# First maxima of an attention block: their keys and queries loaded ahead of block 3's stores, and their visits spread over all remaining projections

## The chip, the cores and the metric

The kernel runs on one core of a Trainium2 chip. The metric is device time in microseconds (us), the median of several runs. Five engines matter: TensorE (PE in the profile, with its weight loads as PEld), VectorE (DVE), ScalarE (ACT), GpSimd (POOL) and SyncE (SP), which here only issues DMAs. Each engine works through its own instructions in order.

## The reference

One transformer block with adaptive layer norm, for 2048 tokens of width 512, 32 heads of width 16:

```
mod = (silu(c) @ w_mod) -> sa, ca, ga, sb, cb, gb
h = layernorm(x) * (1 + ca) + sa
q, k, v = split(h @ wqkv);  p = softmax(q @ k.T / 4) per head
x = x + ga * ((p @ v) @ wo)
h = layernorm(x) * (1 + cb) + sb
x = x + gb * (gelu(h @ w1 + b1) @ w2 + b2)
```

All in float32. A softmax needs for each query the maximum of its scores, and the kernel works these maxima out by matmuls of their own.

## The kernel before, in words

**Parts.** Tokens come in four blocks of 512 (`b`), heads in eight groups of four (`g`); a *unit* `u` is one group with one block of queries, `u = 4 * g + block`. There are three parts. The first (lines 615 to 672) normalises and transposes the blocks and makes the projections of keys and queries of the first 128 channels (`k = 0`: `w = 1` keys, `w = 0` queries) and seven of the sixteen token tiles of values. The second (lines 681 to 755) makes the 33 remaining projections, called *items*: nine value tiles, then `k` = 1 to 3 for each block, keys and queries. In between the matmuls of the items it makes the maxima of the first nine units, in the order of `FRONT` (0, 1, 2, 3, 4, 5, 8, 6, 7). The third part is the attention with the remaining maxima, and after it the feed-forward network. Only the first two parts are edited.

**Projections.** An item is twelve matmuls of line 304 (four chunks, each with high and low parts in three products). `proj_qk` and `proj_v` take a list `fill` of functions that are spread evenly between these twelve. Both return a closure `rest`, which stores the result; it is called later, as the first element of the next item's `fill`. Results go to DRAM (`qk_d`, `v_d`) as high and low parts, and are loaded back in the shape that the scores need.

**Maxima of the front.** For the first nine units keys are not used one by one. For pairs of blocks the kernel stores the sum and the difference of their keys (`kpm_d`, from tiles `pm` and `pmh`, made in `proj_qk` when `pair and b % 2`). The larger of two scores is then |difference| + sum: kind "V" is a matmul with one of the two and an absolute value on ScalarE (line 573), kind "U" a matmul with the other and a combined add and minimum on VectorE (line 576). Both matmuls are line 567, with 48 rows; two row groups (`a` = 0, 1) lie beside each other. Of each unit there are 16 V and 16 U for each row group. `slots` lists them so that a U follows its V, and a *visit* takes three slots, six matmuls. There are 97 visits. The first two units alternate, and their first 16 pairs use only the first half of the keys (blocks 0 and 1).

**Where visits lie.** `FILL0 = 3`: the first three items have none, and the 97 are spread over the other 30, three or four to an item:

```
m, nm = n - FILL0, len(items) - FILL0
fill = [lambda rest=rest: (rest(), visit())] + [visit] * (visits * (m + 1) // nm - visits * m // nm - 1)
```

**Loads.** Keys of the front lie in two tiles `kts[0]` and `kts[1]` (`kt` in the profile), queries in `qmx` (two buffers). Groups 0 and 2 use `kts[0]`, group 1 `kts[1]`: group 2's are loaded at item 19, once group 0 is done. All are loaded by six small DMAs each (`build_k`, line 498; `build_q`, line 509) from SP's queue; in block 3 and the second part the stores go there too (`st[0] = sy`), before that mostly to ScalarE's. The queue is worked in program order, and a DMA that must wait holds up all behind it. The memory of `kts` and `qmx` is that of the input tiles of the first part (`lcm` is closed at block 3), so their loads wait for the last transposes (line 261). `load_qm` of the next unit is issued when the current one is two pairs old, and waits until TensorE has finished with the unit before.

In block 3 the order on SP's queue is: queries of unit 0; block 3's keys; its sum and difference; the first half of the group's keys; queries of unit 1. The second half of the keys follows in items 2 to 4, two DMAs each.

Of the kernel before, what the change touches and what calls it, by code (L numbers as in the profile page):

```python
# [7 lines left out]
F32 = mybir.dt.float32  # L8
# [3 lines left out]
ALU = mybir.AluOpType  # L12
# [5 lines left out]
S = 2048  # L18
# [7 lines left out]
TB = S // NB  # L26
# [9 lines left out]

FRONT = (0, 1, 2, 3, 4, 5, 8, 6, 7, 9)
NU1 = len(FRONT) - 1
FILL0 = 3
VISIT = 3  # L40
OP0 = 1
OPN = 4
# [11 lines left out]
def block_kernel(ctx: ExitStack, tc: tile.TileContext, x, wqkv, wo, w1, b1, w2, b2, c, w_mod, out):  # L54
    nc = tc.nc
    te, ve, ac, gp, sy = nc.tensor, nc.vector, nc.scalar, nc.gpsimd, nc.sync
# [368 lines left out]
    def proj_qk(b, k, w, fill=(), ps=None):  # L425
        hi, lo = hT[b]
        if ps is None:
            ps = bank()
            mm3(ps, [w_hi[k][:, w, i] for i in range(KC)], [w_lo[k][:, w, i] for i in range(KC)],
                [hi[:, i] for i in range(KC)], [lo[:, i] for i in range(KC)], fill)  # L430
        parts = tpool.tile([P, 2, TB], FR, tag="parts", name="parts", bufs=5)
        pair = w and k < 2
        if k or b == 0 or pair and b % 2 == 0:
            raw = tpool.tile([P, TB], F32, tag="raw", name="raw", bufs=3)
            ac.activation(raw, ps, AF.Copy)  # L435
            if pair:
                k2[b % 2] = raw
        if k or b == 0:
            gp.tensor_copy(parts[:, 0], raw)
            gp.tensor_tensor(parts[:, 1], raw, parts[:, 0].bitcast(F32), op=ALU.subtract)  # L440
        else:
            ac.activation(parts[:, 0], ps, AF.Copy)
            ve.tensor_tensor(parts[:, 1], ps, parts[:, 0].bitcast(F32), op=ALU.subtract)
        if pair and b % 2:
            pm = [tpool.tile([P, TB], F32, tag="pm", name="pm", bufs=1), k2[0]]
            pmh = [tpool.tile([P, 2, TB], FR, tag="parts", name="pmh", bufs=5) for _ in range(2)]
            if not k:
                for i, op in enumerate((ALU.add, ALU.subtract)):
                    ve.tensor_tensor(pm[i], ps, k2[0], op=op)
                    ac.activation(pmh[i][:, 0], pm[i], AF.Copy)  # L450

        def pair_store():
            for i in range(2):
                t0 = (b - 1 + i) * TB
                st[0].dma_start(kpm_d[k][:, :, t0 : t0 + TB].rearrange("a p t -> p a t"), pmh[i].bitcast(F32))

        def rest():
            st[0].dma_start(qk_d[w][k][:, :, b * TB : (b + 1) * TB].rearrange("a p t -> p a t"), parts.bitcast(F32))
            if pair and b % 2:
                for i, op in enumerate((ALU.add, ALU.subtract)):  # L460
                    if k:
                        gp.tensor_tensor(pm[i], k2[1], k2[0], op=op)
                        gp.tensor_copy(pmh[i][:, 0], pm[i])
                    eng = gp if k else ve
                    eng.tensor_tensor(pmh[i][:, 1], pm[i], pmh[i][:, 0].bitcast(F32), op=ALU.subtract)
                if k:
                    new.extend([lambda: None, pair_store])
                else:
                    pair_store()

        return rest
# [39 lines left out]
    def load_qm(u):  # L511

        qmx[u] = qmpool.tile([P, 2, TB], FR, tag="qmx", name="qmx", bufs=2)
        build_q(u, qmx[u])
# [105 lines left out]
    rest = lambda: None  # L620
# [8 lines left out]
    for b in range(NB):  # L629
        if b == NB - 1:  # L630
            close(lcm)
            kcm, kpool = pool("kpool")
            kts = [kpool.tile([P, 2, S], FR, name=f"kt{i}") for i in range(2)]
            qmcm, qmpool = pool("qmpool")
            kpm[0], kpm[1] = kts
            load_qm(0)
        if b:
            if b + 1 < NB:
                xn = ln1(b + 1)()
            if b + 2 < NB:  # L640
                load_x(b + 2)
        proj(proj_qk, b, 0, 1, (), None if b else first[1])
        if b == 1:
            load_w(1)
        if b == NB - 1:
            st[0] = sy
            rest()
            rest, st[0] = lambda: None, ac
            build_k(kts[0], kpm_d[0], 0, 0, 2 * TB)
            load_qm(1)  # L650
            split_w(1)
        elif b == 1:
            rest()
            rest = lambda: None
        proj(proj_qk, b, 0, 0, (), None if b else first[0])
        if b == 0:
            xn = ln1(1)()
        if b == NB - 1:
            mod_store(mrow)
            break  # L660
        if b == 1:
            mod_cols(1, mrow)
        for _ in range(V_A[b][0]):
            proj(proj_v, *vitems.pop(0), (), len(vitems) == 15)
        ev = ln1_t(b + 1, xn)
        ev()
        for _ in range(V_A[b][1]):
            proj(proj_v, *vitems.pop(0))
        if b < 2:
            mrow = mod_rows(wms)  # L670
        if b == 0:
            wms = [load_wm(2, 0), load_wm(5, 1)]
# [16 lines left out]
    visits = -(-len(slots) // VISIT)  # L689
# [11 lines left out]
    for n, (k, b, w) in enumerate(items):  # L701
        if n == 1:
            close(acm)
            st[0] = sy
        if 1 < n < 5:
            build_k(kts[0], kpm_d[0], 0, 2 * TB, S, (n - 2,))
        if n == 5:
            load_w(2)
        if n == 7:
            build_k(kts[1], kpm_d[0], 1)  # L710
            for t in kts:
                one_rows(t)
        if n == nv + 1:
            close(vwcm)
            kqcm, kqpool = pool("kqpool")
            kq = [kqpool.tile([P, 2, S], FR, name="kq0")]
            one_rows(kq[0])
            vgcm, vgpool = pool("vgpool", bufs=2)
            qcm, qpool = pool("qpool")
        if n == nv + 2:  # L720
            load_k(0, kq[0])
        if n == nv + 10:
            kpm[2] = kts[0]
            build_k(kts[0], kpm_d[1], 2)
        if n == nv + 15:
            load_v(0)
        if n == nv + 19:
            load_k(2, kts[0])
        if n == nv + 18:
            load_q(0)  # L730
        if n == nv + 20:
            load_q(1)
        if k and b == 1 and w and k < 3:
            split_w(k + 1)
            if k + 2 < 4:
                load_w(k + 2)
        new = []
        fill = [rest]
        if n >= FILL0:
            m, nm = n - FILL0, len(items) - FILL0  # L740
            fill = [lambda rest=rest: (rest(), visit())] + [visit] * (visits * (m + 1) // nm - visits * m // nm - 1)
        if n == len(items) - 1:
            fill += [lambda: None] * 2
        rest = proj_qk(b, k, w, fill) if k else proj_v(b, w, fill)
        for f in todo[:1]:
            f()
        todo = todo[1:] + new
# [386 lines left out]
```

## Time and profile before

| | |
|---|---|
| median of 3 runs | 1742.93 us (1739.42 to 1745.06) |
| the profiled execution | 1743.35 us, span 1741.6 us |
| granted TensorE clock, mean | 0.996 |
| busy | TensorE 99%, VectorE 80%, ScalarE 78%, GpSimd 18% |
| the second part | about 72 to 283 us of the span |

Times in the profile are from the span's start. A row of a timeline gives start, duration, engine, line, operation, what it writes and reads, and a count where several instructions are merged; in brackets how long its engine was idle before it, and what ended that. `SPq` is the queue of SP, and its rows are the issues of DMAs, not their landings. A busy TensorE is not TensorE at its peak: the ends of matmuls are modelled.

### The profile page before, as it was taken

Reading aid. Unit: us, or ns where it says so; the run is one execution under the profiler, and the core shown is the slowest. Engines: PE = TensorE matmul, PEld = TensorE weight load, DVE = VectorE, ACT = ScalarE, POOL = GpSimd, SP = SyncE. Lnnn points to the kernel's source line nnn. Section 1 sums busy time; section 2 is a strip of 40 time slices with the busy share of each in tenths; the row PEclk is TensorE's granted clock in tenths of the full one; section 3 lists DMA queues with packets and bytes.
Section 4 is the critical chain, followed back from the end, with each engine's and each line's share of the span. In section 5 each row is a group of like instructions: output and inputs, shape, how many; then the busy total and the mean of one; then the engine's idle time right before and its main releaser. Section 6 shows DMA issues by size and latency. Waiting matters only on the chain.

```text
span 1741.6 us, 28898 instructions
## 1 busy us (share of the span) xinstructions
PE 1729.5 (99%) x10560; PEld 900.4 (52%) x10560; DVE 1394.6 (80%) x2563; ACT 1351.9 (78%) x2582; POOL 317.4 (18%) x347
## 2 busy tenths in 40 slices
PE   9999999999999999999999999999999999999998
PEld 7655554343433433434343343433433488888887
DVE  6489999898888888888888888888886296746553
ACT  3478888999999999999999999999999732222222
POOL 3205531010000000000000000000013154645562
PEclk9999999999999999999999999999999999999999
DMA  8767657512300400500410111101023064423331
GB/s 305 236 136 166 165 131 149 106 38 43 65 22 19 84 23 23 88 23 24 78 32 24 39 33 26 39 23 36 23 64 102 22 199 125 140 78 116 97 121 49
DMA packets 125218, 144.15 MB, mean 83 GB/s; under 512 B 39026, under 2 KB 74866, under 8 KB 123124
## 3 DMA queue, kind: packets, MB, share of 16 engines
q1 hardware_dynamic: 121620, 135.21, 31.2%
q10 hardware_dynamic: 3456, 7.10, 1.1%
q8 instruction: 83, 1.36, 0.3%
q14 instruction: 59, 0.48, 0.1%
HBM read 106.37 MB, written 35.87 MB: 82 GB/s over the span
## 4 chain that ended last, share of the span: by engine, by line
PE 95%; DVE 2%; DMA 1%; ACT 0%; SPq 0%; POOL 0%; issue 0%; ACTq 0%
PE pv L802 29%; PE mx L548 20%; PE sc L304 15%; PE sc L969 14%; PE mx L1033 6%; PE mx L567 5%; PE pv L1033 2%; PE sc L909 2%; PE mx L909 1%; DMA qk<-parts 0%; PE sc L261 0%; DMA kt<-kpm 0%; PE sc L357 0%; DMA wmod<-in_w_mod_dram 0%; DVE mxs L550 0%; DMA v<-vst 0%
## 5 line engine op out<-in xcount | busy, mean ns | idle before, releaser
L970 ACT ACTIVATE p<-sc 128x512 f32<-128x512 f32 x2048 | 1054.8, 615 | 39.7 <-PE sc L969 13.6
L550 DVE TENSOR_REDUCE mxs<-mx 128x1 f32<-128x512 f32 x1472 | 927.6, 684 | 113.9 <-PE sc L969 79.3
L802 PE MATMUL pv<-p,vg 128*32 128x512 f32 x4096 | 546.0, 605 | 0.0
L969 PE MATMUL sc<-qst,kq 50*128 50x512 f32 x1024 | 284.0, 435 | 0.8 <-ACT raw L435 0.8
L969 PE MATMUL sc<-qst,kt 50*128 50x512 f32 x1024 | 282.4, 431 | 0.0
L548 PE MATMUL mx<-kq,qmx 48*128 48x512 f32 x768 | 262.1, 428 | 0.2
L548 PEld LDWEIGHTS mx<-kq,qmx 48*128 48x128 f32 x768 | 122.6, 184 | 228.6 <-DVE mxs L550 209.3
L548 PE MATMUL mx<-kt,qmx 48*128 48x512 f32 x704 | 239.7, 427 | 0.0
L548 PEld LDWEIGHTS mx<-kt,qmx 48*128 48x128 f32 x704 | 113.2, 184 | 208.3 <-DVE mxs L550 190.7
L1012 ACT ACTIVATE g<-sc,b_c 128x512 f32<-128x512 f32 x56 | 38.6, 690 | 222.7 <-PE sc L304 218.2
L576 DVE CUSTOM_DVE_ANT_0 cp<-mx,cp 128x512 f32<-128x512 f32 x288 | 182.8, 687 | 24.8 <-PE mx L567 21.0
L589 POOL CAST m<-mn 128x16 fp32r<-128x16 f32 x32 | 6.3, 197 | 1016.2 <-DVE mn L583 1016.2
L573 ACT ACTIVATE cp<-mx 128x512 f32<-128x512 f32 x288 | 151.7, 602 | 36.0 <-PE mx L567 35.6
L802 PEld LDWEIGHTS pv<-p,vg 128*32 128x32 f32 x4096 | 81.1, 108 | 180.7 <-issue 169.1
L969 PEld LDWEIGHTS sc<-qst,kq 50*128 50x128 f32 x1024 | 125.7, 185 | 32.9 <-ACT p L970 23.8
L1016 DVE TENSOR_TENSOR glo<-g,ghi 128x512 fp32r<-128x512 f32 x56 | 57.6, 1029 | 92.1 <-ACT ghi L1015 92.1
L969 PEld LDWEIGHTS sc<-qst,kt 50*128 50x128 f32 x1024 | 125.6, 185 | 10.0 <-ACT p L970 3.1
L567 PE MATMUL mx<-kt,qmx 48*128 48x512 f32 x576 | 102.4, 444 | 1.9 <-DMA qmx<-qk 1.7
L838 POOL TENSOR_TENSOR w1l<-w1r,w1h 128x512 fp32r<-128x512 f32 x56 | 76.5, 1366 | 146.7 <-DVE w1h L837 123.1
L840 POOL TENSOR_TENSOR w2l<-w2r,w2h 128x512 fp32r<-128x512 f32 x56 | 82.4, 1472 | 6.2 <-DVE w2h L839 5.8
L567 PEld LDWEIGHTS mx<-kt,qmx 48*128 48x128 f32 x576 | 55.3, 187 | 52.3 <-DVE mxf L576 25.6
L304 PE MATMUL sc<-kt,w1h 128*128 128x512 f32 x224 | 73.8, 391 | 0.0
(175 smaller groups left out, 1667.6 us busy)
## 6 DMA issues: line engine op xcount, KB each, us to landing
w1r<-in_B_w_dram SPq DMA_DIRECT2D x56, 256.0 KB
w2r<-in_B_w_dram SPq DMA_DIRECT2D x56, 256.0 KB
qk<-parts SPq DMA_DIRECT2D x25, 512.0 KB
qmx<-qk SPq DMA_DIRECT2D x192, 64.0 KB
qst<-qk SPq DMA_DIRECT2D x192, 64.0 KB
kq<-qk SPq DMA_DIRECT2D x24, 256.0 KB
kt<-qk SPq DMA_DIRECT2D x24, 256.0 KB
vg<-v SPq DMA_DIRECT2D x8, 664.0 KB
```

The source lines that it names most:

```text
L304: te.matmul(ps, p, q, start=i == 0, stop=i == len(terms) - 1)
L548: te.matmul(ps, qmx[u][rows, p, qc * P : (qc + 1) * P], kst[u // NB][rows, p, kr * TB : (kr + 1) * TB], start=True, stop=True)
L550: ve.tensor_reduce(mxs[u][:, p, a, qc, kr : kr + 1], ps, axis=AX.X, op=ALU.max, negate=True)
L567: te.matmul(ps, qmx[u][rows, p, qc * P : (qc + 1) * P], kpm[u // NB][rows, p, t0 : t0 + TB], start=True, stop=True)
L573: ac.activation(vabs[n, a], ps, AF.Abs)
L576: ve.tensor_tensor_reduce(v, ps, v, -0.5, 3.0e38, ALU.add, ALU.min, mxs[u][:, p, a, qc, r : r + 1])
L802: te.matmul(cur_pv[0][32 * j : 32 * (j + 1)], vg[g][:, kc, j * VW : j * VW + 32], pt.pop((s, j)), start=kc == 0, stop=kc == NKC - 1)
L838: gp.tensor_tensor(alo, a, ahi.bitcast(F32), op=ALU.subtract)
L840: gp.tensor_tensor(blo, b, bhi.bitcast(F32), op=ALU.subtract)
L969: te.matmul(ps, k[r0 : r0 + KX, p, kc * P : (kc + 1) * P], q[r0 : r0 + KX, p], start=True, stop=True)
L970: ac.activation(pb, ps, AF.Exp, scale=SCALE)
L1033: te.matmul(acc[qb][t], p[:, sl], q, start=f == 0 and n == 0, stop=f == NF - 1 and n == 2)
```

## The change

In block 3 the first half of the keys and the queries of unit 1 are loaded directly behind the queries of unit 0, ahead of the block's own projections and stores. The second half of the keys is loaded at once at item 0, six DMAs in a row. The low parts of the sums and differences for `k = 0` are subtracted in `proj_qk` itself and not in `rest`. In block 1 `rest` is no longer called directly after the projection of the keys, but after that of the queries, as elsewhere. `FILL0` is gone: the visits are spread over all 33 items, from item 0 on.

```diff
-FILL0 = 3
...
                 for i, op in enumerate((ALU.add, ALU.subtract)):
                     ve.tensor_tensor(pm[i], ps, k2[0], op=op)
                     ac.activation(pmh[i][:, 0], pm[i], AF.Copy)
+                for i in range(2):
+                    ve.tensor_tensor(pmh[i][:, 1], pm[i], pmh[i][:, 0].bitcast(F32), op=ALU.subtract)
...
             if pair and b % 2:
-                for i, op in enumerate((ALU.add, ALU.subtract)):
-                    if k:
+                if k:
+                    for i, op in enumerate((ALU.add, ALU.subtract)):
                         gp.tensor_tensor(pm[i], k2[1], k2[0], op=op)
                         gp.tensor_copy(pmh[i][:, 0], pm[i])
-                    eng = gp if k else ve
-                    eng.tensor_tensor(pmh[i][:, 1], pm[i], pmh[i][:, 0].bitcast(F32), op=ALU.subtract)
-                if k:
+                        gp.tensor_tensor(pmh[i][:, 1], pm[i], pmh[i][:, 0].bitcast(F32), op=ALU.subtract)
                     new.extend([lambda: None, pair_store])
...
             load_qm(0)
+            build_k(kts[0], kpm_d[0], 0, 0, 2 * TB)
+            load_qm(1)
...
             rest, st[0] = lambda: None, ac
-            build_k(kts[0], kpm_d[0], 0, 0, 2 * TB)
-            load_qm(1)
             split_w(1)
-        elif b == 1:
-            rest()
-            rest = lambda: None
...
-        if 1 < n < 5:
-            build_k(kts[0], kpm_d[0], 0, 2 * TB, S, (n - 2,))
+        if n == 0:
+            build_k(kts[0], kpm_d[0], 0, 2 * TB, S)
...
-        fill = [rest]
-        if n >= FILL0:
-            m, nm = n - FILL0, len(items) - FILL0
-            fill = [lambda rest=rest: (rest(), visit())] + [visit] * (visits * (m + 1) // nm - visits * m // nm - 1)
+        nm = len(items)
+        fill = [lambda rest=rest: (rest(), visit())] + [visit] * (visits * (n + 1) // nm - visits * n // nm - 1)
```

The line numbers of the kernel before are those of the profile before; the changed kernel's differ a little (line 304 becomes 303, 567 becomes 566, 498 becomes 497, 509 becomes 508).

## The prediction

> **What bounds the kernel now.** I read the page first (engines, slices), then a table by stretches, then the timelines of TensorE and of SP's queue around the edit, last the waits. TensorE and VectorE are the candidates:
>
> ```profile
> span 1741.6 us, 28898 instructions
> PE 1729.5 (99%) x10560; PEld 900.4 (52%) x10560; DVE 1394.6 (80%) x2563; ACT 1351.9 (78%) x2582; POOL 317.4 (18%) x347
> ```
>
> The profiled execution took 1743.35 us, its span and 1.75 us around it; the median of the three runs is 1742.93, 0.4 below, so a sum made against the profile stands for the median too. TensorE's 99% is an average. The edit touches the second part, which this table cuts out (columns: stretch, length, busy time and count of TensorE, weight loads, VectorE, ScalarE, GpSimd, granted clock, DMA share, GB/s):
>
> ```profile
> 72.00:80.50 8.50, 8.50 (x37) 6.86 (x37) 1.14 (x2) 2.93 (x6) 2.54 (x2) 1.00 1.05 302
> 80.50:94.83 14.33, 12.45 (x38) 6.77 (x37) 4.20 (x13) 6.25 (x12) 0.00 (x0) 0.64 0.82 186
> 118.96:242.67 123.71, 123.71 (x595) 72.55 (x594) 118.05 (x380) 104.86 (x204) 54.95 (x68) 1.00 0.64 157
> 283.43:1741.00 1457.57, 1452.48 (x9216) 726.11 (x9216) 1159.04 (x1860) 1153.37 (x2210) 226.95 (x211) 1.00 0.25 62
> ```
>
> The second part is 33 projections ("items", 12 matmuls of line 304 each) from 72.0 to 283.4. In its first 8.5 us VectorE does 1.14 us of work; in the next 14.3 TensorE is idle for 1.9 and its clock falls; from 119 to 243 VectorE is busy 118.05 of 123.71 and TensorE all of it. So both engines are near their limit in the steady state, and the start is wasted on both. Everything after 283.4 is untouched by the edit and only moves.
>
> The timeline of TensorE gives the prices:
>
> ```profile
> 72.01 2.13 PE L304 MATMUL sc<-wv,hThi 128*128 128x512 f32 x8
> ...
> 80.51 1.10 PE L304 MATMUL sc<-wv,hThi 128*128 128x512 f32 x4
> 83.34 0.47 PE L567 MATMUL mx<-kt,qmx 48*128 48x512 f32 x1 [1.73 <-DMA qmx<-qk]
> 83.96 0.80 PE L567 MATMUL mx<-kt,qmx 48*128 48x512 f32 x2 [0.16 <-DMA kt<-kpm]
> 84.69 2.07 PE L304 MATMUL sc<-wv,hThi 128*128 128x512 f32 x4
> 86.69 1.65 PE L567 MATMUL mx<-kt,qmx 48*128 48x512 f32 x6
> ...
> 93.85 1.05 PE L567 MATMUL mx<-kt,qmx 48*128 48x512 f32 x6
> ```
> ```profile
> 111.21 0.97 PE L304 MATMUL sc<-wv,hThi 128*128 128x512 f32 x3
> ...
> 118.96 1.21 PE L304 MATMUL sc<-wv,hThi 128*128 128x512 f32 x4
> 120.09 0.96 PE L567 MATMUL mx<-kt,qmx 48*128 48x512 f32 x6
> ...
> ```
> ```profile
> 230.26 1.20 PE L304 MATMUL sc<-hThi,w 128*128 128x512 f32 x4
> ...
> 248.78 0.97 PE L304 MATMUL sc<-hThi,w 128*128 128x512 f32 x3
> ...
> 282.23 1.20 PE L304 MATMUL sc<-hTlo,w 128*128 128x512 f32 x4
> 284.20 0.83 PE L969 MATMUL sc<-qst,kq 50*128 50x512 f32 x3 [0.77 <-ACT raw L435]
> ```
>
> An item without maxima takes (80.51 - 72.01) / 3 = 2.83 us. One with three visits (a visit is six matmuls of line 567) takes (248.78 - 230.26) / 3 = 6.17, so a visit adds 1.11 on TensorE. One with four takes 118.96 - 111.21 = 7.75, not the 2.83 + 4 x 1.11 = 7.28 of TensorE: there VectorE, at 1.94 per visit, is the limit. Three visits are TensorE's case, four are VectorE's.
>
> **The change, part by part.** *Visits.* Before, 97 visits lie on 30 items, three each and four on seven of them. Now they lie on all 33: three on 31, two on items 0 and 16, no four. On TensorE: item 0 has only half of its first visit (three matmuls), 2.83 + 0.55 + 1.11 = 4.5; 30 items of 6.17 are 185.1; item 16 2.83 + 2.22 = 5.05; the last, with VectorE's tail behind it, 6.5. Sum 201.2. Before, the stretch 72.01 to 283.43 took 211.4. So the gain, with nothing in the way, is **10.2 us**: 1.9 of idle at the start; 4.0 of half clock (from 84.69 to 93.85 TensorE did 12 matmuls of line 304 and 12 of line 567, which at the steady 1.13 per four and 0.92 per six are 5.2, not 9.2); the remaining 4.3 is the better spreading.
>
> *First keys and queries ahead of the stores.* SP's queue before:
>
> ```profile
> 62.15 3.48 SPq L509 DMA_DIRECT2D qmx<-qk  x6
> 69.77 0.38 SPq L458 DMA_DIRECT2D qk<-parts  x1
> 71.76 1.08 SPq L455 DMA_DIRECT2D kpm<-pmh  x2
> 72.93 4.81 SPq L498 DMA_DIRECT2D kt<-kpm  x6
> 77.78 4.80 SPq L509 DMA_DIRECT2D qmx<-qk  x6
> ```
> ```profile
> SPq L509 <- PE sc L261: 1.7, 1, 1.7
> ```
>
> The keys stood behind stores that wait for block 3's parts until 72.5. The first queries waited only for the transposes (line 261) that read the memory they take over; the keys need the same release, so now they go out behind them, from 65.6. The first visit comes after six matmuls of item 0, at 72.01 + 6 x 0.236 = 73.4. How long the six key loads take is the first unknown: before, 72.93 to 83.96 is 11.0, but with three stores of 512 KB in front of them in the queue. Alone they need 2.7 us of issuing (as in the row at 193.58 below) and a landing. With the loads in rotation behind the queries, whose own issuing took 3.48, I take 7.5 to 8, landing at 73 to 73.7, a wait of 0.3; bounds 0 (landing before 73.4) and 76.7 - 73.4 = 3.3.
>
> *Stores and second half of the keys.* Block 3's stores move back behind the keys and the second queries, by about 6 to 8 us, and the six loads of the second half, now in one batch in item 0, wait for them. Nothing needs that half before the eleventh visit, in item 3 at about 95. Before, they went out singly between the stores of items 0 to 2, and were in when the DMA first fell quiet:
>
> ```profile
> 92.00:94.00 2.00, 2.00 (x6) 1.16 (x6) 1.06 (x4) 1.17 (x3) 0.00 (x0) 0.50 0.07 8
> ```
>
> Behind the later stores I estimate them in at about 92 too (stores at 79, 5.5 to the loads as at 188.05 below, then half of the 15.6 of a whole load). Taken at nothing; if the 3 us of margin are gone, each us late is a us of TensorE. The VectorE subtractions move from the store's closure to the projection: same order on VectorE, since nothing stood between; nothing. The extra flush in block 1 goes: its store on ScalarE's queue comes one projection later in block 1, and is read in block 3; nothing. On ScalarE the store of item 0's predecessor now stands ahead of the first absolute values and waits for VectorE until 73.98: 0.6 us for ScalarE, hidden by six free banks.
>
> *What becomes late next.* Maxima now run ahead of projections: by eight visits at item 3, falling to none at the end. Every load whose source is a projection keeps its place among the items, while its reader comes earlier. The tightest is the keys of the third group, which reuse the first group's tile, read from visit 64 on:
>
> ```profile
> 158.04 3.15 SPq L509 DMA_DIRECT2D qmx<-qk  x6
> ...
> 161.75 1.38 SPq L455 DMA_DIRECT2D kpm<-pmh  x2
> ...
> 188.05 1.41 SPq L455 DMA_DIRECT2D kpm<-pmh  x2
> 193.58 2.66 SPq L498 DMA_DIRECT2D kt<-kpm  x6
> ```
> ```profile
> SPq L498 <- DMA kpm<-pmh: 4.1, 1, 4.1
> ...
> SPq L509 <- DMA kt<-kpm: 3.3, 2, 1.7
> ```
> ```profile
> 194.00:207.00 13.00, 13.00 (x62) 7.43 (x60) 12.47 (x41) 11.26 (x23) 6.92 (x10) 1.00 1.02 121
> ```
> ```profile
> 209.16 0.32 SPq L509 DMA_DIRECT2D qmx<-qk  x1
> ```
> ```profile
> 218.41 1.20 PE L304 MATMUL sc<-hThi,w 128*128 128x512 f32 x4
> 219.54 0.50 PE L567 MATMUL mx<-kt,qmx 48*128 48x512 f32 x2
> ```
>
> The store is issued at 188.05, the keys at 193.58 after 4.1 us of waiting for it, six loads of 256 KB that fill the DMA (share 1.02) at 121 GB/s for 13 us; a later query load that waited for the last of them goes at 209.16, 15.6 us after the first issue. The reader, visit 64, starts at 219.5: 10 us to spare. In the changed order of SP's queue the six query loads of unit 8 stand ahead of this store, where before they stood behind the keys, and they wait until TensorE has finished with the fifth unit's queries, whose buffer they take, in visit 54. From there: queries 3.15, store to keys 5.5, keys 13.6 to the fifth load (all that one row group needs) and 15.6 to the sixth: 22.3 and 24.3. From visit 54 to visit 64 TensorE needs ten visits at 6.17 / 3, less the part of visit 54 already done: 20.2. The first reader waits some 1.6 us (22.3 against 20.2, half a us off because the store has no 512 KB in front of it now), and, three matmuls (0.6) later, the second row group 1.4 more. I take **3.0 us**, in two pieces; bounds 0 (the store lands at once) and 4.5 (each step as slow as its slowest row). By the same count the queries of the fifth unit, now behind the first attention keys (kq, six loads of the same size), come about when visit 42 asks for them: 0.3, bounds 0 and 1.5.
>
> The Trainium skill would price the key load otherwise: "DMA: Bandwidth & Descriptors", Bandwidth, lists 1 MB in 6.15 us, 341 GB/s. By that 1.57 MB are an estimated 4.6 us, nothing is late, and the sum is the no-stall case below. The row's 121 GB/s disagrees, and the sum goes by the row.
>
> **Sum:** 1743.35 - 10.2 + 0.3 + 0.3 + 3.0 = 1736.7.
>
> **Rivals.** *A: the stall also halves the clock.* The trace has one pair of cases:
>
> ```profile
> 46.30:49.70 3.40, 2.00 (x18) 1.77 (x16) 1.11 (x4) 1.09 (x2) 0.00 (x0) 1.00 1.08 361
> 80.40:83.80 3.40, 1.67 (x7) 0.81 (x5) 0.00 (x0) 0.60 (x1) 0.00 (x0) 1.00 0.97 154
> ```
>
> With 1.4 us idle in 3.4 the clock stayed; after 1.73 in 3.4 it was halved. Each piece of the new stall is near 1.4, the two together are not; if both fall into one such stretch, 4.0 us more: 1740.7. The Trainium skill, "TensorE: Matmul & The Clock Gate", What's actually happening, has this as a free-running window of 3413 ns, which the two rows fit; it speaks against the change, and makes A a matter of phase between executions.
>
> *B: no stall at visit 64.* If the store lands sooner (4.1 us of waiting had other stores in front) and the loads overlap better, the keys are there: 1743.35 - 10.2 + 0.6 = 1733.8. Against it: the 13 us at full DMA share.
>
> *C: the change doesn't bring the first keys early, and it ends slower.* One place: item 0. If the six loads take the 11.0 us of before they land at 76.7; TensorE waits 3.3 there instead of 0.3, and the clock halves, 4.0. With the stall at visit 64: 1736.7 + 3.0 + 4.0 = 1743.7, and each us later adds one; if a load must also wait for a store of ScalarE's, as the keys at 188 waited for theirs, an estimated 2 (half of that 4.1) more, 1745.7. From a landing at 76.4 on the stall and the clock eat the whole gain. Together with A's clock at visit 64 it is 1747.7 to 1749.7. For it: the only measured time of this load. Against: the stores that made it slow now come after it.
>
> **Chances.** The forecast 0.40, A 0.27, B 0.21, C 0.12. Faster by over 0.3% (about what a measurement of this kernel can tell from no change), below 1737.7: all of B, 0.7 of the forecast (its own spread is some 1.8 us), a little of A: 0.51. Slower by over 0.3%, above 1748.2: C with A's clock, about 0.05, and 0.01 for what I haven't seen: 0.06. Same 0.43. Range 1732.5 (B, with a us of error) to 1744.0 (A, with its stall at the bound of 4.5, and the milder half of C). The forecast's own range is 1734.5 to 1739.
>
> **What would show it.** The first matmul of line 566 (567 before) at 73 to 74 with no idle of over 0.5 us before it and the clock at 1.00 between 84 and 94: the start is right. Items with three visits at 6.1 to 6.2 and the last L304 at about 276.5: the sum. An idle of TensorE of 1 to 2 us released by the DMA kt<-kpm at about 207: the late keys; if it is absent, B; if the clock is 0.5 after it, A. If items with three visits are slower than 6.17, because VectorE never gets its slack back, the whole of the 4.3 us of spreading is wrong; a wait at about 95 or 161 would be the margins that I put at nothing.

## The result, and the profile after

| | before | after |
|---|---|---|
| median, 17 executions each | 1742.93 us (1737.59 to 1751.30) | 1757.73 us (1745.25 to 1769.46) |
| the profiled execution | 1743.35 us, span 1741.6 | 1758.06 us, span 1756.2 |
| granted TensorE clock, mean | 0.996 | 0.987 |

The change makes the kernel slower: the ratio of the times is 1.0082, 95% interval [1.0059, 1.0105]. The forecast was 1736.7 us and its range ended at 1744.0. After's own spread is 24 us, and it follows the clock: its fastest execution (1745.25) had a mean clock of 0.996, its slowest (1769.46) one of 0.981.

The head of the page of after:

```profile
span 1756.2 us, 28900 instructions
PE 1741.6 (99%) x10560; PEld 907.7 (52%) x10560; DVE 1395.9 (79%) x2563; ACT 1352.2 (77%) x2582; POOL 317.8 (18%) x347
```

TensorE is again busy for 99%. Its busy time grew by 12 us with the same 10560 matmuls: the matmuls themselves became longer. The table by stretches of after says where (same columns as for before; the clock is the third value from the end):

```profile
72.00:80.50 8.50, 7.47 (x32) 4.36 (x33) 3.74 (x11) 6.02 (x13) 2.51 (x2) 1.00 0.76 212
80.50:94.83 14.33, 14.33 (x72) 8.73 (x71) 13.47 (x43) 11.92 (x24) 0.00 (x0) 1.00 0.84 211
118.96:242.67 123.71, 118.75 (x507) 69.80 (x506) 98.14 (x313) 87.72 (x169) 50.45 (x60) 0.86 0.67 152
...
164.56:171.39 6.83, 6.52 (x18) 3.68 (x20) 2.80 (x9) 2.66 (x5) 1.90 (x5) 0.50 0.95 345
171.39:215.76 44.37, 42.30 (x207) 25.66 (x207) 38.78 (x123) 34.86 (x67) 24.81 (x27) 1.00 0.60 136
215.76:253.31 37.55, 37.52 (x107) 20.45 (x104) 20.42 (x65) 18.16 (x35) 6.17 (x9) 0.50 0.35 117
...
300.00:1756.00 1456.00, 1451.39 (x9216) 725.53 (x9216) 1158.21 (x1856) 1152.83 (x2209) 227.12 (x211) 1.00 0.25 62
```

The start is as wanted: from 80.50 to 94.83, where before had a clock of 0.64 and 38 matmuls, after has 1.00 and 72. The attention behind 300 us is unchanged (1456 us for 9216 matmuls; before 1457.57). The loss lies in the stretch from 119 to 243: 507 matmuls instead of 595. Its clock was halved twice, for 6.83 us and for 37.55 us.

What stands ahead of each half clock, and what it does to the matmuls, in the timeline of TensorE of after:

```profile
74.59 1.01 PE L566 MATMUL mx<-kt,qmx 48*128 48x512 f32 x3 [1.02 <-DMA kt<-kpm]
```
```profile
161.27 0.73 PE L566 MATMUL mx<-kt,qmx 48*128 48x512 f32 x4
164.87 0.79 PE L566 MATMUL mx<-kt,qmx 48*128 48x512 f32 x2 [2.87 <-DMA qmx<-qk]
```
```profile
212.14 1.20 PE L303 MATMUL sc<-hThi,w 128*128 128x512 f32 x4
215.41 2.09 PE L566 MATMUL mx<-kt,qmx 48*128 48x512 f32 x6 [2.07 <-issue]
217.43 2.07 PE L303 MATMUL sc<-hThi,w 128*128 128x512 f32 x4
219.43 1.65 PE L566 MATMUL mx<-kt,qmx 48*128 48x512 f32 x6
221.00 2.07 PE L303 MATMUL sc<-hTlo,w 128*128 128x512 f32 x4
```

The wait at the start (1.02 us) leaves the clock alone. The one in visit 42 (2.87 us, for the fifth unit's queries) and the one at visit 64 (2.07 us, for the third group's keys) are each followed by a half clock. From then on four projection matmuls and a visit take 221.00 - 217.43 = 3.57 us, an item with three visits 10.7 instead of the 6.17 of the prediction. SP's queue of after shows why the loads were late:

```profile
144.04 4.28 SPq L497 DMA_DIRECT2D kq<-qk  x6
148.37 0.97 SPq L163 DMA_DIRECT2D wraw<-in_A_wqkv_dram  x2
150.59 0.37 SPq L459 DMA_DIRECT2D qk<-parts  x1
152.73 8.62 SPq L508 DMA_DIRECT2D qmx<-qk  x6
...
```
```profile
193.15 2.66 SPq L508 DMA_DIRECT2D qmx<-qk  x6
195.86 0.94 SPq L456 DMA_DIRECT2D kpm<-pmh  x2
201.03 2.65 SPq L497 DMA_DIRECT2D kt<-kpm  x6
```
```profile
SPq L508 <- DMA kq<-qk: 22.3, 14, 1.8
```

The six query loads of the fifth unit (152.73) stand behind the attention keys kq and take 8.62 us to be issued, because they wait for landings of kq (last row, the waits of SP's queue over the whole execution: us in total, times, longest; 8.1 us in five waits lie between 150 and 162). In the kernel before they stood behind kq too, but 19.0 us behind and not 8.7, and were issued in 3.15 us (158.04, in the prediction). The row of kq before:

```profile
139.05 2.75 SPq L498 DMA_DIRECT2D kq<-qk  x6
```

The third group's keys go out at 201.03; TensorE asks for them at 213.34 (212.14 + 1.20), 12.3 us later, and its matmuls start at 215.41. The profile names no releaser for that wait (`issue`); that it ends with the keys is read from these times and from the runs below, where it goes when the keys are loaded earlier.

The account of the profiled execution: 4.9 us of waits, and 6.83 + 37.55 = 44.4 us of half clock, in which 1 - 6.17 / 10.7 = 0.42 of each us is lost, 18.8. Together 23.7. Without them it would have taken 1734.4. The half clocks before the last few us of the kernel are, in all profiles kept, multiples of one length of 3.41 us: 6.83 us is two of it, 10.24 three, 37.55 eleven. Such a length is called a *window* below.

### The profile page after: what moved, and what is told of

Read it like the earlier page. It is cut to its first block, busy times and chain, and to the rows that moved or that the text cites. A ratio compares the mean times of both kernels' runs of the same rounds, so it can differ in the third digit from the quotient of the medians.

```text
span 1756.2 us, 28900 instructions
## 1 busy us (share of the span) xinstructions
PE 1741.6 (99%) x10560; PEld 907.7 (52%) x10560; DVE 1395.9 (79%) x2563; ACT 1352.2 (77%) x2582; POOL 317.8 (18%) x347
## 4 chain that ended last, share of the span: by engine, by line
PE 94%; DVE 2%; DMA 2%; POOL 0%; issue 0%; ACT 0%; SPq 0%; ACTq 0%; POOLq 0%; DVEq 0%
PE pv L796 29%; PE mx L547 20%; PE sc L303 14%; PE sc L963 13%; PE mx L1027 6%; PE mx L566 5%; PE pv L1027 2%; PE sc L903 2%; PE mx L903 1%; DMA qk<-parts 1%; DMA kq<-qk 1%; PE pv L343 0%; DMA qmx<-qk 0%; PE sc L260 0%; PE sc L356 0%
## 5 line engine op out<-in xcount | busy, mean ns | idle before, releaser
L547 PE MATMUL mx<-kt,qmx 48*128 48x512 f32 x704 | 239.8, 427 | 0.0
L566 PE MATMUL mx<-kt,qmx 48*128 48x512 f32 x576 | 106.1, 465 | 6.0 <-DMA qmx<-qk 2.9
L303 PE MATMUL sc<-hThi,w 128*128 128x512 f32 x240 | 77.4, 450 | 0.7 <-DVE hThi L266 0.7
```

The lines of the kernel that those rows point to most:

```text
L303: te.matmul(ps, p, q, start=i == 0, stop=i == len(terms) - 1)
L547: te.matmul(ps, qmx[u][rows, p, qc * P : (qc + 1) * P], kst[u // NB][rows, p, kr * TB : (kr + 1) * TB], start=True, stop=True)
L566: te.matmul(ps, qmx[u][rows, p, qc * P : (qc + 1) * P], kpm[u // NB][rows, p, t0 : t0 + TB], start=True, stop=True)
```

## The experiments

**Theory:** the spread of the visits and the early loads are right, and two loads that come some 2 us late each start a half clock whose length (6.83 and 37.55 us here) decides the time. **Rivals:** the denser order is itself too much for VectorE or for the clock; or the waits only move to the next load. All ratios are to the kernel before, run on the same chip; its medians there were 1743.75 to 1745.06 us.

### Both loads in time

```diff
-                    new.extend([lambda: None, pair_store])
+                    new.extend([pair_store])
...
-        if n == nv + 2:
+        if n == nv + 3:
             load_k(0, kq[0])
-        if n == nv + 10:
+        if n == nv + 9:
             kpm[2] = kts[0]
```

> The changed kernel, but both late loads issued sooner: the attention keys kq one item later, so that the fifth unit's queries stand ahead of them on SP's queue; the third group's sums and differences stored one item earlier and its keys loaded one item earlier. Theory: the whole loss is two stalls of TensorE at visits 42 and 64 and the half clock behind them. Taking the items' excess (24.5 us) off the profiled 1758.06 gives 1733.6 us, within 2; granted clock 0.999 or more; no wait of a matmul of line 566 over 1 us except the one at the start; the spread between executions under 4 us. Rival: the visits spread over all items are themselves too dense, the clock falls or items grow without any stall: 1750 or more, items of three visits above 6.3 us or a half clock with no wait in front. Second rival: the stalls only move to another load (the second queries, the attention keys): 1740 to 1750 with a new wait of 1 to 3 us named in the waits.

Measured: 1735.37 us (1734.27 to 1738.03), ratio 0.9954 [0.9936, 0.9971]. The same loads on SP's queue, the dense stretch, and the start:

```profile
147.35 3.19 SPq L508 DMA_DIRECT2D qmx<-qk  x6
150.58 2.98 SPq L497 DMA_DIRECT2D kq<-qk  x6
```
```profile
188.97 2.66 SPq L497 DMA_DIRECT2D kt<-kpm  x6
```
```profile
118.96:242.67 123.71, 123.71 (x604) 74.65 (x600) 116.07 (x371) 103.61 (x200) 56.73 (x68) 1.00 0.71 168
```
```profile
74.71 0.49 PE L566 MATMUL mx<-kt,qmx 48*128 48x512 f32 x1 [0.40 <-DMA kt<-kpm]
75.49 0.49 PE L566 MATMUL mx<-kt,qmx 48*128 48x512 f32 x2 [0.29 <-DMA kt<-kpm]
```

The queries go out 5.4 us sooner and in 3.19 us, the keys 12 us sooner. TensorE has no idle time in the dense stretch, and 604 matmuls fit into it (before 595). No wait has taken the place of the two. The rivals fall: the density costs nothing that shows here, and the change with its two loads moved beats the kernel before.

### Only the early loads

```diff
+FILL0 = 3
...
-        nm = len(items)
-        fill = [lambda rest=rest: (rest(), visit())] + [visit] * (visits * (n + 1) // nm - visits * n // nm - 1)
+        fill = [rest]
+        if n >= FILL0:
+            m, nm = n - FILL0, len(items) - FILL0
+            fill = [lambda rest=rest: (rest(), visit())] + [visit] * (visits * (m + 1) // nm - visits * m // nm - 1)
```

> The changed kernel with the visits spread as before (none in the first three items, 97 over the other 30): only the early loads are left. Theory: the idle of 1.9 us and the half clock of 4.0 us at the start of the kernel before go and nothing else changes: 1743.35 - 5.9 = 1737.4 us, clock 0.999, no stall at visits 42 and 64, because the maxima run less far ahead; spread under 4 us. Rival: moving the stores behind the loads costs by itself (late second half of the keys): a wait at about 95 us and 1743 or more.

Measured: 1737.82 us (1736.64 to 1740.36), ratio 0.9966 [0.9950, 0.9982]. The early loads are worth the idle and half clock that they remove at the start; no new wait appears. The spread of the visits brings the remaining 2.4 us of the kernel with both loads in time.

### One load late at a time

Queries in time, keys late: only the edit of `nv + 3` above.

> Only the first of the two repairs: kq one item later, the third group's keys as late as in the changed kernel. Theory: no stall at visit 42, the stall of 2 us at visit 64 stays and halves the clock for a stretch whose length differs between executions (windows of 3.41 us, between 1 and 12 of them, because at half clock a visit with its four projection matmuls takes 3.58 us and a window holds two idle switches in most phases): 1733.6 + 2 + 0.456 us per us of half clock, that is 1737 to 1754, a mean of some 1745.6, the time of each execution following its mean clock. Rival 1: the length follows the size of the stall and is the same each time: one value, 1752, in all executions. Rival 2: half clock lasts two or three windows as a rule and the 11 windows were chance: 1739 to 1741 in nearly all executions.

Keys in time, queries late: only the edits of `pair_store` and `nv + 9`.

> Only the second repair: the third group's sums and keys an item earlier, kq as in the changed kernel. Theory: the stall of 2.9 us at visit 42 stays, the one at visit 64 goes; the half clock behind visit 42 again lasts 1 to 12 windows, not always the two of the profiled execution: 1738 to 1755, mean some 1746. Rival 1 (length given by the place or by the stall): 1733.6 + 5.9 = 1739.5 in all executions. Rival 2: taking away the later stall changes nothing since the wait moves to visit 64 by another load: 1755 or more.

Measured: with the keys late 1747.97 us (1738.54 to 1757.00), ratio 1.0017 [0.9994, 1.0041]; with the queries late 1746.97 (1740.83 to 1754.02), ratio 1.0008 [0.9986, 1.0029]. Their profiled executions, first the keys late, then the queries late:

```profile
205.85:209.26 3.41, 1.84 (x12) 1.12 (x9) 2.00 (x8) 2.06 (x4) 1.02 (x2) 1.00 0.92 118
209.26:236.56 27.30, 27.25 (x77) 14.76 (x77) 14.67 (x47) 12.90 (x25) 5.05 (x7) 0.50 0.39 128
236.56:287.76 51.20, 51.20 (x245) 30.34 (x246) 47.98 (x153) 42.30 (x82) 16.04 (x20) 1.00 0.64 155
291.18:308.24 17.06, 17.06 (x65) 6.35 (x64) 9.05 (x16) 9.75 (x20) 0.72 (x1) 0.50 0.94 136
```
```profile
163.24:166.65 3.41, 1.04 (x5) 0.74 (x6) 0.98 (x3) 0.76 (x2) 1.87 (x2) 1.00 0.93 236
166.65:183.72 17.07, 17.07 (x49) 9.69 (x49) 8.37 (x29) 7.49 (x16) 4.70 (x7) 0.50 0.53 178
```

Each late load alone costs its wait and a half clock: eight windows of 3.41 us in the one, five in the other. The execution with the keys late has a second half clock, of five windows, from 291.18 to 308.24, where the attention begins; if each us loses 0.42 there too, it is an estimated 7 of its 1756.02 us, and neither of the two loads is near it. The executions of one kernel spread over 13 to 18 us and follow their clock (keys late: 1738.54 at 0.998, 1757.00 at 0.987). So the length isn't given by the size of the stall: a wait of 2.87 us had two windows behind it in the changed kernel, one of 1.57 us (3.41 - 1.84 in the first row above) eight in the one with the keys late. That refutes the rivals of these runs, which wanted nearly one time for every execution, or 1755 us and more. How much of the spread belongs to the second place isn't known, since one profile of each kernel is kept.

### A plain item behind the stall

Queries in time, keys late, and in addition:

```diff
+        nvis = visits * (n + 1) // nm - visits * n // nm
+        if n == 23:
+            nvis = 0
+        if n in (29, 30, 31):
+            nvis += 1
```

> The kernel with only the queries in time (one stall of some 2 us at visit 64 left), and the item after that stall, item 23, without visits; its three go to items 29 to 31, which then have four. Theory: at half clock the alternation of four projection matmuls and one visit has a period of 3.58 us, so that nearly every 3.41 us window holds two switches and with them a little idle time, and the clock comes back only when the phase is right; twelve to sixteen projection matmuls in a row (6 to 8 us at half clock) hold a window without any switch, so the clock is back within item 23 or at the start of item 24: the half clock of this stall never exceeds five or six windows (17 to 20 us) where it reached eight in the profiled execution before; the time is 1735.4 + 2 + 1.5 (four-visit items at VectorE's pace, 7.75 instead of 6.17 + 1.11) + 0.456 x 3 to 20: 1740 to 1748, highest below 1750, median some 1743.5. Rival 1 (the length doesn't depend on the pattern of matmuls): the same spread of 18 us as without the plain item, up to 1757. Rival 2 (work load decides: three items' visits at the end make a stall or half clock of their own): half clock near 260 to 290.

Measured: 1745.06 us (1739.47 to 1746.75), ratio 0.9986 [0.9958, 1.0013]. The profiled execution:

```profile
212.83:216.24 3.41, 3.41 (x11) 1.99 (x10) 1.92 (x6) 1.57 (x3) 0.00 (x0) 0.50 0.70 216
216.24:219.65 3.41, 3.41 (x11) 1.96 (x10) 2.03 (x7) 2.06 (x4) 0.00 (x0) 0.50 0.00 0
219.65:223.07 3.42, 3.42 (x9) 2.65 (x9) 0.01 (x1) 0.00 (x0) 1.89 (x2) 0.50 0.14 51
223.07:226.48 3.41, 3.41 (x18) 2.01 (x17) 1.45 (x5) 2.12 (x4) 1.90 (x2) 1.00 0.47 137
```

```profile
218.33 3.78 PE L303 MATMUL sc<-hThi,w 128*128 128x512 f32 x8
221.91 1.62 PE L303 MATMUL sc<-hTlo,w 128*128 128x512 f32 x4
```

The half clock lasts four windows, from 209.41 to 223.07; the table shows the last three. Two windows with a mix of both kinds of matmul are busy all through and stay at half clock; the next, from 219.65, holds projection matmuls alone (the timeline below the table), and the clock is back behind it. The highest time is 10 us lower than without the plain item, as expected; the median is 1.5 over what I had expected. This profile speaks for the matmuls' pattern and against the first rival. The times alone don't show it: an estimated 7 us of the slow execution without the plain item came from the half clock at 291.18, and here the one at that place (287.92) lasted only one window. Whether the edit shortened that one too, or chance did, is open. The second rival gains nothing from it, since the kernel with the queries late has a half clock there too (289.53 to 292.94).

### Matmuls in the waits

The changed kernel, with twelve useless matmuls ahead of each waiting one:

```diff
+        if kind == "V" and a == 0 and n in (64, 96):
+            dps = bank_mx()
+            for i3 in range(12):
+                te.matmul(dps, hT[3][0][:, 0, :P], hT[3][0][:, i3 % KC], start=True, stop=True)
```

> The changed kernel with its late loads, and twelve full projection-size matmuls more (their result is not used) ahead of each of the two waiting matmuls, at visits 42 and 64; 24 matmuls of 0.236 us, 5.7 us of work that nobody needs. Theory: the waits are filled, TensorE is never idle over some 0.5 us, the clock stays: 1735.4 (both loads in time) + 5.7 + rest waits of 0 to 0.5 = 1741 to 1741.6, granted clock 0.998 or more, spread below 5 us: 16 us faster than the changed kernel although it does more. Rival 1: what lowers the clock is not the idle time but the dense mix of matmuls or the DMA load there: 1757.7 or more with half clock at 165 and 216 as before. Rival 2: late loads hold more than the first matmul (further waits behind): between, with waits of over 1 us left behind the added matmuls.

Measured: 1742.27 us (1740.69 to 1747.71), ratio 0.9986 [0.9964, 1.0009].

```profile
160.00:168.00 8.00, 8.00 (x39) 5.00 (x37) 4.60 (x15) 4.04 (x8) 1.90 (x2) 1.00 0.98 304
208.00:216.00 8.00, 8.00 (x40) 5.50 (x39) 5.04 (x18) 4.51 (x9) 1.90 (x2) 1.00 0.95 238
```

The loads are as late as in the changed kernel and the DMA is as full, but TensorE is busy in both places and keeps its clock. With 24 matmuls more the median falls from 1757.73 to 1742.27. So most of what the changed kernel pays is the clock, and what lowers the clock is the wait of TensorE, not the dense mix of matmuls or the DMA load.

### What a window must hold

Queries in time, keys late, and four visits in a row behind the stall:

```diff
+        nvis = visits * (n + 1) // nm - visits * n // nm - (n in (23, 24, 25))
+        fill = [lambda rest=rest: (rest(), visit())] + [visit] * (nvis - 1)
+        if n == 22:
+            fill[0] = lambda rest=rest: (rest(), visit(), visit(), visit(), visit())
```

> The kernel with only the queries in time (one stall at visit 64), and the four visits 64 to 67 directly behind each other in item 22, with visits 68 and 69 after them as usual; items 23 to 25 have two visits instead of three and at most six projection matmuls in a row (3.0 us at half clock, less than a window). It tells apart what a window of 3.41 us must hold for the clock to come back. Theory 1 (no switch between the two kinds of matmul in the window): 24 matmuls of 48 rows, 6.3 us at half clock, hold a window without a switch in most phases, so the clock is back within one to three windows in most executions: 1735.4 + 2 + 0.456 x 3.4 to 10, 1739 to 1742 in most, median below 1742, few above 1745. Theory 2 (enough matmuls that use all 128 rows in the window; those of 48 rows count for little): the four visits bring nothing, the spread stays that of the kernel with the queries in time, 1738.5 to 1757, median near 1748. In both, VectorE falls behind by up to 1 us at the end of the four visits.

Measured: 1745.10 us (1740.82 to 1749.25), ratio 0.9994 [0.9968, 1.0019], which neither theory gave. The profiled execution, by the matmuls of line 303 (128 rows, *wide* below) and then of line 566 (48 rows, *narrow* below):

```profile
209.02:212.43 3.41, 0.00 (x0) 0.00 (x0) 1.00 1.06 398
212.43:215.84 3.41, 0.06 (x1) 0.06 (x1) 0.50 0.79 255
215.84:219.26 3.42, 2.02 (x4) 1.10 (x4) 0.50 0.00 0
```
```profile
209.02:212.43 3.41, 2.76 (x13) 1.37 (x12) 1.00 1.06 398
212.43:215.84 3.41, 3.41 (x12) 1.96 (x10) 0.50 0.79 255
215.84:219.26 3.42, 1.49 (x7) 0.83 (x6) 0.50 0.00 0
```

The window from 212.43 is full of narrow matmuls, all but 0.06 us at its end, and the clock stayed at half. It came back after a window with four wide ones. That speaks against my theory of switches and for the other, that wide matmuls count. The shorter spread may then come from a part of the edit that I had thought harmless, six wide matmuls in a row, 3.0 us at half clock, in items 23 to 25; no run tests that. And the window from 209.02 lost the clock with only 0.65 us idle, but no wide matmul.

The changed kernel, with narrow matmuls in the waits instead of wide ones (18 and 14, on keys and queries of the unit before):

> The changed kernel with its late loads, and matmuls of 48 rows (18 at visit 42, 14 at visit 64, on the keys and queries of the unit before; result not used) ahead of the two waiting matmuls in place of nothing: 32 x 0.153 = 4.9 us of work that nobody needs. Theory 1 (any matmul keeps the clock, only idle time costs it): 1735.4 + 4.9 + rest waits of 0 to 0.5 = 1740.3 to 1741, a little less than with the 24 full matmuls (1742.3), clock 0.998, spread as there. Theory 2 (a stretch with matmuls of 48 rows alone counts as partly idle): the clock falls at 165 and 216 as in the changed kernel: 1750 to 1762.

Measured: 1745.83 us (1742.28 to 1758.80), ratio 0.9997 [0.9966, 1.0028]. A mixture: six executions of twelve lie at 1742.3 to 1745.2, at a clock of 0.997 or more, the slowest five at 1750.7 to 1758.8 with 0.995 to 0.989. These narrow matmuls took 0.217 us each (sixteen from 162.11 to 165.58) rather than 0.153, since they use only one row group (in both, 48 of them took 5.73 us in a run below, 0.119 each), so the sum without half clock is 1742.3, where the fastest lie. The profiled execution is the fastest, and it kept its clock although no wide matmul ran from 161.53 to 166.57, 5.0 us; some of the narrow ones there ran in both row groups at once. So narrow matmuls alone don't halve the clock each time. The next three runs go on from there. They have both loads in time and add, at visit 48 where nothing waits, a stretch of useless work: 32 narrow matmuls, 32 wide ones, or 48 narrow ones alternating between the row groups.

```diff
+        if kind == "V" and a == 0 and n == 72:
+            dps = bank_mx()
+            for i3 in range(32):
+                te.matmul(dps, qmx[u][rows, 0, :P], kpm[u // NB][rows, 0, i3 % 4 * TB : (i3 % 4 + 1) * TB],
+                          start=True, stop=True)
```

> Both loads in time (1735.4), and at visit 48, where nothing waits, 32 added matmuls of 48 rows in one row group, in a row, result not used: 32 x 0.217 = 6.9 us, the same step as in the narrow filling of the waits. TensorE has no idle time there. Theory A (only idle time lowers the clock): 1735.4 + 6.9 = 1742.3, clock 0.999, spread under 4 us. Theory B (a window of 3.41 us needs enough work on all 128 rows, and idle time is only one way to miss it): 6.9 us of narrow work hold such a window in every execution, so the clock halves each time without any wait, for 3 to 41 us: 1744 to 1761, median some 1750.

> The control: 32 added matmuls of 128 rows at the same place, 32 x 0.236 = 7.5 us. Both theories: 1735.4 + 7.5 = 1742.9, no half clock, spread under 4 us.

> 48 added matmuls of 48 rows at the same place, alternating between the two row groups as a visit does, two of them side by side: 48 x 0.153 = 7.3 us, up to 96 rows at work at a time. Theory A: 1742.7, clock 0.999. Theory B, counting rows at work: between; if 96 of 128 rows are enough for a full clock, 1742.7 with a spread under 4 us; if a narrow matmul counts as 48 rows whatever runs beside it, as with the single row group, 1744 to 1761.

| added | median (range), us | ratio |
|---|---|---|
| 32 narrow | 1753.91 (1743.99 to 1763.68) | 1.0053 [1.0027, 1.0079] |
| 32 wide | 1742.70 (1740.72 to 1761.11) | 1.0002 [0.9973, 1.0031] |
| 48 narrow in pairs | 1740.63 (1739.60 to 1749.91) | 0.9983 [0.9956, 1.0009] |

The 32 narrow ones:

```profile
176.87:180.28 3.41, 3.41 (x17) 2.77 (x16) 0.00 (x0) 0.00 (x0) 3.27 (x4) 1.00 0.41 154
180.28:183.69 3.41, 3.41 (x11) 2.65 (x11) 0.00 (x0) 0.00 (x0) 1.04 (x1) 0.50 0.00 0
...
211.00:214.40 3.40, 3.40 (x16) 2.07 (x18) 2.87 (x9) 2.34 (x5) 3.24 (x4) 1.00 0.67 195
```

TensorE is busy for the whole window from 176.87, waits for nothing, and its clock is halved at 180.28, for 30.7 us. No execution of this kernel kept a clock above 0.998, and all but the fastest lie above 1747. The times don't say where in each execution the clock was lost; the profile does for one. The wide control gave its sum in ten of twelve executions (1740.7 to 1743.3). Its profiled execution is its slowest, 1761.11, with a half clock of seven windows from 77.36 on, 108 us ahead of the added work, and one of six windows from 295.81 on, behind it; the clock was 1.00 during the added work. Its waits (us in total, times, longest) name the first keys:

```profile
PE mx L570 <- DMA kt<-kpm: 1.4, 2, 1.0
```

In pairs, up to 96 rows at work, the narrow matmuls gave their sum (48 in 5.73 us, from 175.70 on, so 1741.1) in nine of twelve. The times agree with theory B for one row group. The comparison with the pairs is weaker than it looks, because their stretch is shorter (5.73 us against 6.9) and so fills fewer windows; why two side by side usually pass, and what halves the clock in the other three, stays open.

### The first bank of the attention

Both loads in time, and `set_rings(sc=(1, 2, 3, 0), ...)` in place of `(0, 2, 3, 1)` ahead of the third part.

> Both loads in time, and the third part takes its first score bank from the one that is long free (order 1, 2, 3, 0 instead of 0, 2, 3, 1): the 0.77 us that the first score matmul of line 963 waits for the copy of the last projection goes. Theory: that wait, together with the small gaps beside it, halves the clock for one or more windows in some executions (the upper group of the times of both loads in time, 1737 to 1738); without it only the lower group remains: 1733.5 to 1734.5 in nearly all executions. Rival 1: the wait moves to the fourth score matmul, which then takes bank 0: no change of the median (1735.4). Rival 2: the upper group has another origin (the start wait of 0.7 us): the median falls by 0.8 only and the two groups stay.

Measured: 1734.95 us (1733.88 to 1737.01), ratio 0.9942 [0.9920, 0.9963].

```profile
274.07 1.20 PE L303 MATMUL sc<-hTlo,w 128*128 128x512 f32 x4
275.20 0.50 PE L963 MATMUL sc<-qst,kq 50*128 50x512 f32 x2
```

The 0.77 us ahead of the first score matmul is gone. The lower group of times fell to 1733.9 to 1735.0, but five executions still lie at 1735.9 to 1737.0: the second rival is nearest, and the origin of the upper group is open. This is the fastest kernel measured here; against both loads in time alone, its 0.4 us is within the intervals.

## Why the prediction was wrong

- **The sum of the visits was right.** 10.2 us of gain, with nothing in the way, is 1733.15. Both loads in time gives 1734.27 in its profiled execution, with 0.7 us of waiting at the start. The split is rougher: by the profiled executions the early loads alone bring 1743.35 - 1736.91 = 6.4 us where I had 5.9, and the spreading 1736.91 - 1734.27 + 0.7 = 3.3 where I had 4.3.
- **The first keys** came at 74.6 and cost 1.02 us instead of 0.3, without a loss of clock in the profile of after: in the bounds. Case C didn't happen there; in the run with 32 wide matmuls two waits at this place, 1.4 us together, were followed by a half clock of 23.9 us, so what it describes does occur.
- **The wait at visit 64** was foreseen at 3.0 in two pieces and came as 2.07 in one. Place, mechanism and chain were right: from the issue of unit 8's queries to the first matmul of visit 64 it is 215.41 - 193.15 = 22.3 us, and TensorE was there after 213.34 - 193.15 = 20.2, the two numbers of the prediction; the second piece of 1.4 didn't come. The two pieces were what kept the forecast apart from rival A: "Each piece of the new stall is near 1.4, the two together are not". One piece of 2.07 in one window is A. The estimate of 4.6 us for the key load goes by the 341 GB/s that the prediction quotes from the Trainium skill, "DMA: Bandwidth & Descriptors", Bandwidth; by the 6.15 us for 1 MB quoted beside it, the estimate is 9.7 us. By neither would the keys be late, so the argument there is the same.
- **The wait in visit 42** was put at "0.3, bounds 0 and 1.5" and was 2.87. I had counted the kq loads ahead of the queries as a matter of order, "come about when visit 42 asks for them", without working out their chain: the queries had stood behind kq before as well, but now follow it by 8.7 us instead of 19.0, and their issues take 8.62 us, since they wait for landings of kq.
- **The step that failed most is the half clock behind a late load.** The sum holds nothing for it, because the stall was to come in two pieces that leave the clock alone; rival A prices it at "4.0 us more". That price was taken from the one event in the profile of before, three windows long. In the changed kernel's profiled execution two events cost 18.8. The number in the row was correct; that it was one draw from a wide distribution was not seen. The kernel before shows the width itself: of the runs beside the experiments its fastest is 1738.17 at a clock of 1.000, so without the half clock that its profile has at the start, and its slowest 1758.91 at 0.987; where that one lost its clock isn't known. The three times of before, 5.6 us apart, already spoke against a fixed 4.0. It also means that 4.0 of the 10.2 us of gain are what one execution of before paid, and that the executions of before at a full clock (1738 to 1740) leave less to gain.

Why the length varies has a reading from the rows, which no run tests by itself. At half clock the pattern of four projection matmuls and one visit has a period of 3.57 us, and the windows are 3.41 long: the half clocks seen here last between 1 and 11 times that (1: 284.11 to 287.52 in the last row of this document; 3: 83.82 to 94.06 in before; 11: 215.76 to 253.31 in after). From one window to the next the pattern moves by only 0.16 us. A window in which a wide matmul is cut short stays at half clock, and the next one looks almost the same; up to 2.0 / 0.16 = 12 windows pass until the four wide ones lie in one window. That the clock comes back sooner with 12 or 6 wide matmuls in a row agrees. It isn't exact: in the profile of before a window with all four (87.2 to 90.6) didn't bring the clock back, and the ends of matmuls are modelled, so that the last of the eleven windows (from 249.90) shows the same cut of 0.16 us as those before it.

The Trainium skill, "TensorE: Matmul & The Clock Gate", What's actually happening, gives the full clock back "After ≥1 busy SHORT window (~3.4µs sustained)". The length of the windows agrees with the rows here. The rule doesn't: from 215.76 to 253.31 TensorE was busy for 37.52 of 37.55 us, eleven such windows, at half clock; and in the run with 32 narrow matmuls a window (176.87 to 180.28) busy for 3.41 of 3.41 took the clock away. The rows decide.

## What to carry to other kernels

When work is moved forward, follow each load that it reads back through its queue, with what its issues wait for, and move the load by as many steps as its reader; here one load put an item later, out of the way of another, and one put an item earlier turned a loss of 0.8% into a gain of 0.5%. A stall of some 2 us on TensorE can cost, beside its 2 us, a half clock of very different length (here up to 37.55 us), so price it as a distribution, from several executions, never from one profile, and ask of the kernel before what its own spread contains. Where a wait can't be avoided, wide matmuls in it limited the damage here; a run of wide ones behind it did so in one profile.

## What the runs showed that I had not expected

A busy TensorE can lose its clock: narrow matmuls (48 rows, one row group) alone, 3.41 us of 3.41, were followed by a half clock at 180.28. The end of the second part is a place of this sort too: seven of the fourteen profiles kept have a half clock that begins between 284 and 296, of one window in five of them, of five and six windows in the other two (keys late, and 32 wide matmuls). It occurs with late loads and without, and adds a spread of its own to the times above. In the run with four visits in a row the window ahead of a half clock at 284.11 holds only 0.17 us of idle time:

```profile
280.70:284.11 3.41, 3.24 (x17) 2.07 (x21) 2.59 (x8) 2.82 (x7) 2.26 (x4) 1.00 0.03 7
284.11:287.52 3.41, 3.41 (x15) 1.16 (x7) 1.79 (x4) 2.26 (x5) 0.00 (x0) 0.50 0.99 250
```

It is there that the last projections end and score and maxima matmuls of 50 and 48 rows follow each other. What exactly the window counts, rows at work or something near it, and where its limits lie, these runs don't settle.
